# Sliding-window attention woven into a chain of matrix products: all of a group's attention products moved into one place

## The chip, the cores and the metric

The kernel runs on one core of a Trainium2 chip. The metric is the device time of one execution in microseconds (us). The core has five engines with queues of their own: PE (TensorE, the matrix products; the trace lists its weight loads apart, as PEld), DVE (VectorE), ACT (ScalarE), POOL (GpSimd) and SP (SyncE, which here only issues transfers). An engine takes its instructions in the order in which the program wrote them, and waits at one until what it needs is there.

## What is computed

The reference, cut to what matters:

```python
# q, k, v: (4, 8, 576, 64); window 64
scores = q @ k.T / 8
scores = where((rel >= 0) & (rel < 64), scores, -1e9)
attn = exp(scores - max); attn = attn / (sum(attn) + 1e-9)
x = (attn @ v)                      # as (2304, 512)
x = ((x @ w1) * (x @ w2) @ w3) @ w_out          # d_ff 1024
h = x @ w_in; out = (h * sigmoid(h)) @ w_out2   # d_ff 2048
```

## The kernel before

The 2304 tokens are 18 blocks of 128 queries, and the 8 heads are 4 pairs: 72 groups of attention, one for 128 queries and two heads. Three blocks of queries make a block of 384 tokens for the products that follow, of which there are six.

A group goes through these steps. `load_qk` and `load_v` have SP fetch its operands. `prep_qk` and `prep_v` (ACT, POOL, DVE) split them into a high and a low part in fp32r; the first 17 groups (`plain`) skip this and multiply in fp32. `scores` is three products on PE (one for a plain group) into the one PSUM tile `s`, followed by two reductions on DVE (line 275, which also mask). `exps` is two exponentials on ACT (line 286). `normalise` is three DVE operations (lines 294, 296, 298). `transposes` is three products on PE into the one PSUM tile `t` (line 308). `split_t` takes them out of PSUM: one ACT copy (line 314) for a plain group, else two kinds of ACT casts and two kinds of DVE subtractions (lines 318 to 323). `values` is three products on PE (lines 335 to 337, or 343 and 344) into the PSUM tile `o`, after which the result goes to the tile `xr`: one ACT copy (line 338) for a plain group, else two ACT copies, two DVE additions and one POOL addition (lines 347 to 351).

`half(h)` issues half a group's work: the even half 2g and the odd half 2g+1. The halves are spread over the other work by hand: `phase_w` (weights are converted from 64-bit words and `w3 @ w_out` is formed, PE line 476) issues the first 28 between its matrix products, and `phase_a` (the products `ab`, line 504, and `x`, line 524) issues one before each unit of 12 products, 24 units for each block of 384 tokens. So one group comes every two units. In `phase_w` steps of the conversion stand between the halves (`steps_to`), and `fill` puts single conversion steps of DVE between a half's own.

`split_x(blk, c)` makes the high and low parts of a fourth of `xr` (three groups) for the products of the next block; in `phase_a` it is called after the halves of units 17, 19, 21 and 22, and from the second block on both of its operations are DVE's. SP's transfers stand in one order too: a `load_v` that waits for a buffer holds up the loads of weight words (line 107) behind it.

The last phases (the products `h` and `o` of the second feed-forward network) hold no attention.

Of the kernel before, what the change touches and what calls it, by code (L numbers as in the profile page):

```python
# [9 lines left out]
F32 = mybir.dt.float32  # L10
# [4 lines left out]
ALU = mybir.AluOpType  # L15
# [27 lines left out]
def tile_window_attention_ffn(ctx, tc, qkv, vp, mask, ident, w1, w2, w3t, w_out, w_in, w_out2, out):  # L43
# [7 lines left out]
    nc = tc.nc  # L51
# [4 lines left out]
    att = late.enter_context(tc.tile_pool(name="att", bufs=2, side="right"))  # L56
    psa = late.enter_context(tc.tile_pool(name="psa", bufs=1, space=PSUM))

    def f32(ap):
        return ap.bitcast(F32)  # L60
# [91 lines left out]
    def loads_to(n):  # L152
        while done["load"] < min(n, len(line)):
            if line[done["load"]]:
                line[done["load"]].load()
            done["load"] += 1
# [29 lines left out]


    NG = NU * NPAIR
    LAST_HALF = 2 * NG + 2
    qk_raw, v_raw, qk_st, v_st, s_st, p_st = {}, {}, {}, {}, {}, {}  # L190
    pt = {}

# [9 lines left out]
    def plain(g):  # L202


        return g < PLAIN

    def place(g):
        blk, r = divmod(g, 3 * NPAIR)
        return blk * 3 + r % 3, r // 3
# [90 lines left out]
    def transposes(g):  # L300

        x = sm[g % 2]
        t_ps = psa.tile([128, 384], F32, name=f"t{g}", tag="t")
        x = x.rearrange("p h n -> p (h n)")
        for i, at in enumerate((0, 256, 128)):
            nc.tensor.transpose(t_ps[:, i * 128 : i * 128 + 128], x[:, at : at + 128], id_sb)  # L308
        return t_ps

    def split_t(g, t_ps):
        if plain(g):
            p_st[g] = p_w[g % 2]
            nc.scalar.copy(out=p_st[g], in_=t_ps[:, 0:320])
            return
        b, a = pt[g % 2, 1], pt[g % 2, 0]
        own, before = t_ps[:, 0:256].rearrange("p (h n) -> p h n", h=2), t_ps[:, 256:320]
        nc.scalar.copy(out=b[:, :, 0, :], in_=own)
        for h, hs in HEADS:
            nc.scalar.copy(out=a[hs, h, 0], in_=before[hs])  # L320
        nc.vector.tensor_tensor(out=b[:, :, 1, :], in0=own, in1=f32(b[:, :, 0, :]), op=ALU.subtract)
        for h, hs in HEADS:
            nc.vector.tensor_tensor(out=a[hs, h, 1], in0=before[hs], in1=f32(a[hs, h, 0]), op=ALU.subtract)

    def values(g):
        u, c = place(g)
        r = u % 3 * 128

        tag = "z" if done["step"] == len(line) and g % 2 else "o"
        o_ps = psa.tile([128, 2, 2, 128], F32, name=f"o{g}", tag=tag)  # L330
        if plain(g):


            v, p, o = v_p[g % 3], p_st.pop(g), o_ps[:, 0, 0]
            nc.tensor.matmul(o, lhsT=v[:, 0:128], rhs=p[:, 0:128], start=True, stop=False)
            nc.tensor.matmul(o, lhsT=v[:, 64:192], rhs=p[:, 128:256], start=False, stop=False)
            nc.tensor.matmul(o[:, 0:64], lhsT=v[:, 192:320], rhs=p[:, 256:320], start=False, stop=True)
            nc.scalar.copy(out=xr[:, c, r : r + 128], in_=o)
            return
        vhl = v_st.pop(g)  # L340
        b, a = pt[g % 2, 1], pt[g % 2, 0]
        for h in range(2):
            nc.tensor.matmul(o_ps[:, h], lhsT=vhl[:, h], rhs=b[:, h], start=(h == 0), stop=False)  # L343
        nc.tensor.matmul(o_ps[:, :, :, 0:64], lhsT=vhl[:, 2], rhs=a, start=False, stop=True)  # L344
        o_ps = o_ps.rearrange("p h t n -> p h (t n)")
        t = att.tile([128, 256], F32, name=f"ot{g}", tag="ot", bufs=1)
        nc.scalar.copy(out=t[0:64], in_=o_ps[64:128, 0, :])
        nc.scalar.copy(out=t[64:128], in_=o_ps[0:64, 1, :])
        nc.vector.tensor_tensor(out=t[0:64], in0=o_ps[0:64, 0, :], in1=t[0:64], op=ALU.add)
        nc.vector.tensor_tensor(out=t[64:128], in0=o_ps[64:128, 1, :], in1=t[64:128], op=ALU.add)  # L350
        nc.gpsimd.tensor_tensor(out=xr[:, c, r : r + 128], in0=t[:, 0:128], in1=t[:, 128:256], op=ALU.add)  # L351

    def half(h):


        g, odd = divmod(h, 2)
        if not odd:
            t_ps = transposes(g - 1) if 1 <= g <= NG else None
            if g < NG:
                scores(g)  # L360
            if t_ps is not None:
                split_t(g - 1, t_ps)
            if g < NG:
                exps(g)
        else:
            if g < NG:
                normalise(g)
            if 1 <= g <= NG:
                values(g - 1)
            for x in (g + 1, g + 2):  # L370
                if x - g == (1 if plain(x - 2) else 2):
                    prep_qk(x)
            if g < NG:
                prep_v(g)

            for x in range(g + 2, g + 5):
                if g < (x - 2 if plain(x - 2) else x - 4):
                    break
                load_qk(x)
            for x in range(g + 1, g + 4):  # L380
                if g < (x - 2 if plain(x - 3) else x - 3):
                    break
                load_v(x)

    halves = [0]

    def halves_to(n):
        while halves[0] < min(n, LAST_HALF):
            half(halves[0])
            halves[0] += 1  # L390
# [10 lines left out]
    def phase_w():  # L401
# [57 lines left out]
        acc, split_done = {}, set()  # L459
        for s in range(16):  # L460
            sw, j = divmod(s, 8)
            loads_to(ready[s + 2] + (3 if s > 1 else 0))
            if j == 0:
                for i in range(4):
                    acc[i] = accumulator(f"accw{sw}_{i}", [128, 512])
            for part in range(2):
                first = ready[s + 1 if s else 0]
                steps_to(first + (ready[s + 2] - first) * (part + 1) // 2, (nc.vector, nc.gpsimd), 3)
                halves_to(min(W_HALVES, 2 + W_HALVES * (2 * s + part + 1) // 32))
                for c in range(4):  # L470
                    if halves[0] >= 6 * c + 8 and (0, c) not in split_done:
                        split_done.add((0, c))
                        split_x(0, c)
                fill(3)
                for i in (0, 1) if part == 0 else (2, 3):
                    nc.tensor.matmul(  # L476
                        acc[i], lhsT=w3x[s % 7][:, i * 128 : (i + 1) * 128], rhs=wo[:, j],
                        start=(j == 0), stop=(j == 7),
                    )
                    if j == 7:  # L480
                        n = sw * 4 + i
                        wp[n] = slot(f"wp{n}", f"w{16 + n}", [2, 512], F32R)
                        split(wp[n][:, 0], wp[n][:, 1], acc[i], "act", "dve")
# [58 lines left out]
    with tc.manual_schedule():  # L542
        xr = slot("xr", "xr", [4, NB])
# [39 lines left out]
        for first, last in ((0, 3), (3, 7), (7, 11), (11, 16)):  # L583
# [6 lines left out]
            for key, src in chunks:  # L590
                tag = tags.pop(0)
# [68 lines left out]
        for i in range(1, len(jobs) + 1):  # L660
            if i < len(jobs):
                j, f = jobs[i]
# [93 lines left out]
```

## Time and profile before

| | |
|---|---|
| median of the runs | 884.69 us (the other near it: 883.5) |
| the profiled execution | 884.13 us, span 882.3 us |
| granted TensorE clock, mean | 0.997 of full speed |
| PE busy | 856.0 us (97% of the span) |
| DVE, ACT, POOL busy | 480.7, 491.0, 430.6 us |

The time outside the span is 884.13 - 882.3 = 1.8 us. The first weights and operands arrive at some 7 us; `phase_w` with its 28 halves lasts to about 104 us, the five blocks with attention to about 425 us, and the sixth block and the second network make up the rest. Busy shares are means over these stages, which have different limits.

### The profile page before, as it was taken

What the parts mean: (1) busy time and instruction counts of PE and PEld (TensorE: products, weight loads), DVE (VectorE), ACT (ScalarE), POOL (GpSimd) and SP (SyncE); (2) the same over time, 40 slices, a digit from 0 to 9 for tenths busy, and PEclk for the clock granted to TensorE, in tenths of its full rate; (3) what the DMA queues carried; (4) which work ended last, traced back from release to release, by engine and by line L of the source; (5) the groups of instructions that cost most, each with busy time, mean ns of one, the idle gap of its engine ahead of it and who ended that gap; (6) DMA issues with size and microseconds to landing.
All of it is one profiled execution on the core that took longest, in us unless ns stands there. A gap on an engine that the chain in (4) does not pass through costs nothing.

```text
span 882.3 us, 13255 instructions
## 1 busy us (share of the span) xinstructions
PE 856.0 (97%) x4362; PEld 737.0 (84%) x4362; DVE 480.7 (54%) x1202; ACT 491.0 (56%) x1219; POOL 430.6 (49%) x474
## 2 busy tenths in 40 slices
PE   4998999999999999999999999999999999999997
PEld 2454689999999999999999888888888888888896
DVE  5889888878888888888365886111111111111111
ACT  5778677788787788787475775222222222222322
POOL 4558476466466466465395787222322232222222
PEclk9999999999999999999999999999999999999999
DMA  8888423333432323331477500200020001000100
GB/s 286 295 251 262 134 79 99 125 99 100 127 94 90 126 90 100 119 99 50 182 277 261 202 0 1 77 20 0 1 89 7 0 1 51 22 0 1 48 1 25
DMA packets 43205, 85.84 MB, mean 97 GB/s; under 512 B 4864, under 2 KB 22528, under 8 KB 43136
## 3 DMA queue, kind: packets, MB, share of 16 engines
q1 hardware_dynamic: 37088, 75.55, 26.4%
q10 hardware_dynamic: 6048, 9.44, 2.9%
q8 instruction: 35, 0.57, 0.3%
q14 instruction: 34, 0.28, 0.1%
HBM read 75.53 MB, written 9.44 MB: 96 GB/s over the span
## 4 chain that ended last, share of the span: by engine, by line
PE 86%; DVE 2%; POOL 1%; issue 1%; ACT 0%; DMA 0%; POOLq 0%; SPq 0%; DVEq 0%
PE h L627 23%; PE o L646 22%; PE ab L504 21%; PE x L524 11%; PE t L308 2%; PE o L343 2%; PE s L265 1%; PE s L269 1%; PE accw L476 1%; PE o L344 1%; POOL klo L244 1%; DVE cv_b L128 0%; DVE cv_z L125 0%; DVE rs L294 0%; PE s L261 0%
## 5 line engine op out<-in xcount | busy, mean ns | idle before, releaser
L82 POOL TENSOR_TENSOR g<-sg,g 128x512 fp32r<-128x512 f32 (+1 forms) x80 | 94.8, 1185 | 250.0 <-ACT g L79 237.3
L627 PE MATMUL h<-x2t,hl 128*128 128x512 f32 (+1 forms) x960 | 213.4, 371 | 0.0
L646 PE MATMUL o<-hl,g 128*128 128x512 f32 x864 | 211.2, 392 | 0.4 <-ACT g L79 0.3
L633 DVE TENSOR_TENSOR sg<-h,sg 128x512 f32<-128x512 f32 (+1 forms) x80 | 51.1, 638 | 288.5 <-ACT sg L632 288.5
L627 PEld LDWEIGHTS h<-x2t,hl 128*128 128x128 f32 x960 | 169.4, 188 | 33.8
L646 PEld LDWEIGHTS o<-hl,g 128*128 128x128 f32 x864 | 160.9, 188 | 35.9 <-ACT g L79 0.8
L632 ACT ACTIVATE sg<-h 128x512 f32<-128x512 f32 (+1 forms) x80 | 44.4, 555 | 195.4 <-PE h L627 195.4
L504 PE MATMUL ab<-xa,hl 128*128 128x384 f32 x576 | 117.1, 338 | 0.0
L504 PE MATMUL ab<-xb,hl 128*128 128x384 f32 x576 | 115.6, 335 | 0.0
L504 PEld LDWEIGHTS ab<-xb,hl 128*128 128x128 f32 x576 | 101.4, 188 | 0.0
L504 PEld LDWEIGHTS ab<-xa,hl 128*128 128x128 f32 x576 | 99.8, 188 | 0.8
L351 POOL TENSOR_TENSOR xr<-ot 128x128 f32<-128x128 f32 x55 | 33.2, 603 | 118.5 <-DVE ot L350 116.5
L132 POOL TENSOR_TENSOR cv_b<-cv_b,cv_r 128x512 int32<-128x512 int32 x48 | 73.6, 1534 | 26.8 <-DVE cv_b L128 11.2
L79 ACT CAST g<-sg 128x512 fp32r<-128x512 f32 (+1 forms) x80 | 46.3, 579 | 63.5 <-DVE sg L633 61.8
L286 ACT ACTIVATE sm<-sm,nm 128x192 f32<-128x192 f32 x144 | 64.4, 448 | 17.7 <-DVE nm L275 16.6
L244 POOL TENSOR_TENSOR klo<-qk,qkhi 64x192 fp32r<-64x192 f32 x110 | 70.1, 637 | 5.7 <-ACT qkhi L240 1.5
L524 PE MATMUL x<-p,wp 128*128 128x384 f32 x360 | 69.6, 335 | 0.0
L524 PEld LDWEIGHTS x<-p,wp 128*128 128x128 f32 x360 | 62.2, 188 | 0.1
L125 DVE TENSOR_SCALAR cv_z<-cv_b 128x512 int32<-128x512 int32 x72 | 49.4, 686 | 17.0 <-ACT cv_b L114 16.6
L114 ACT ACTIVATE cv_b<-words 128x512 f32<-128x512 f32 x72 | 48.2, 670 | 11.5 <-DMA words<-in_w_out 5.6
L128 DVE SCALAR_TENSOR_TENSOR cv_b<-words,cv_z 128x512 int32<-128x512 int32 x72 | 49.4, 686 | 3.5 <-issue 0.5
L275 DVE CUSTOM_DVE_ANT_0 sm<-s,mask_sb 128x192 f32<-128x192 f32 x144 | 45.7, 354 | 6.6 <-PE s L261 3.6
(82 smaller groups left out, 1258.9 us busy)
## 6 DMA issues: line engine op xcount, KB each, us to landing
qk<-in_qkv SPq DMA_DIRECT2D x55, 384.0 KB, 3.1
words<-in_w_out SPq DMA_DIRECT2D x24, 512.0 KB, 8.4
words<-in_w3t SPq DMA_DIRECT2D x16, 512.0 KB, 6.2
words<-in_w SPq DMA_DIRECT2D x16, 512.0 KB, 6.2
words<-in_w_in SPq DMA_DIRECT2D x16, 512.0 KB, 6.8
v<-in_qkv SPq DMA_DIRECT2D x55, 96.0 KB, 2.7
x2d<-x2s ACTq DMA_DIRECT2D x24, 192.0 KB, 1.9
out_x<-osb ACTq DMA_DIRECT2D x18, 256.0 KB, 2.1
```

Of the source, the lines that this page charges most:

```text
L82: (nc.vector if eng_lo == "dve" else nc.gpsimd).tensor_tensor(out=lo, in0=src, in1=f32(hi), op=ALU.subtract)
L114: nc.scalar.activation(out=f32(self.b), in_=f32(self.high), func=AF.Copy, scale=2.0**-112)
L125: nc.vector.tensor_scalar(out=self.z, in0=b, scalar1=3, scalar2=None, op0=ALU.logical_shift_left)
L128: nc.vector.scalar_tensor_tensor(out=b, in0=self.high, scalar=-0x80000000, in1=self.z, op0=ALU.bitwise_and, op1=ALU.bitwise_or)
L132: nc.gpsimd.tensor_tensor(out=x, in0=b, in1=self.r, op=ALU.add)
L244: nc.gpsimd.tensor_tensor(out=k_lo[g % 2][hs, h * 192 : h * 192 + 192], in0=t[hs, n], in1=f32(hi[hs, n]), op=ALU.subtract)
L286: nc.scalar.activation(out=x, in_=x, func=AF.Exp, scale=-1.0, bias=nm[:, h : h + 1], accum_out=rs[:, h : h + 1])
L504: nc.tensor.matmul(acc, lhsT=w[:, l, fs], rhs=x[k // 2][:, k % 2, r, :], start=(k == 0 and n == 0), stop=(k == 3 and n == 2),)
L524: nc.tensor.matmul(acc, lhsT=wp[f][:, l, o * 128 : (o + 1) * 128], rhs=p[f][:, r, :], start=(f == 0 and n == 0), stop=(f == 7 and n == 2),)
L627: nc.tensor.matmul(acc, lhsT=weights["in", f // 4, k][:, l, fs], rhs=x[:, k, r, :], start=(k == 0 and i == 0), stop=(k == 3 and i == 2),)
L633: nc.vector.tensor_tensor(out=sg, in0=acc, in1=sg, op=ALU.mult)
L646: nc.tensor.matmul(oacc[t], lhsT=g[:, l, t * 128 : (t + 1) * 128], rhs=weights["out", f][:, r, :], start=(f == 0 and i == 0), stop=(f == 1 ...
```

## The change

In the even half 2g the order becomes: the values' products of group g-2, the scores of group g, the transposes of group g-1. `values` no longer issues what takes its result out of PSUM but gives it back as a function, which the half calls behind `split_t` and ahead of `exps`. The odd half has no products left. Values of a group come one half later than before, so there is one half more in all, a `load_v` of a plain group is issued one group later, and `split_x` in `phase_w` is called one half later.

```diff
-    LAST_HALF = 2 * NG + 2
+    LAST_HALF = 2 * NG + 3
@@ values(g)
-            nc.scalar.copy(out=xr[:, c, r : r + 128], in_=o)
-            return
+            return lambda: nc.scalar.copy(out=xr[:, c, r : r + 128], in_=o)
...
+        def total():
+            t = att.tile([128, 256], F32, name=f"ot{g}", tag="ot", bufs=1)
+            nc.scalar.copy(out=t[0:64], in_=o_ps[64:128, 0, :])
+            nc.scalar.copy(out=t[64:128], in_=o_ps[0:64, 1, :])
+            nc.vector.tensor_tensor(out=t[0:64], in0=o_ps[0:64, 0, :], in1=t[0:64], op=ALU.add)
+            nc.vector.tensor_tensor(out=t[64:128], in0=o_ps[64:128, 1, :], in1=t[64:128], op=ALU.add)
+            nc.gpsimd.tensor_tensor(out=xr[:, c, r : r + 128], in0=t[:, 0:128], in1=t[:, 128:256], op=ALU.add)
+
+        return total
@@ half(h)
         if not odd:
-            t_ps = transposes(g - 1) if 1 <= g <= NG else None
+            out_of = values(g - 2) if 2 <= g <= NG + 1 else None
             if g < NG:
                 scores(g)
-            if t_ps is not None:
-                split_t(g - 1, t_ps)
+            if 1 <= g <= NG:
+                split_t(g - 1, transposes(g - 1))
+            if out_of is not None:
+                out_of()
             if g < NG:
                 exps(g)
         else:
             if g < NG:
                 normalise(g)
-            if 1 <= g <= NG:
-                values(g - 1)
...
-                if g < (x - 2 if plain(x - 3) else x - 3):
+                if g < (x - 1 if plain(x - 3) else x - 3):
                     break
                 load_v(x)
@@ phase_w
-                    if halves[0] >= 6 * c + 8 and (0, c) not in split_done:
+                    if halves[0] >= 6 * c + 9 and (0, c) not in split_done:
```

On PE, near the start of a block's units in `phase_a` (`t` transposes, `s` scores, `o` values, `ab` the unit's products), there stood before:

```order
L504 MATMUL ab_14_2442<-xa_1644,hl 128x384 x6
L504 MATMUL ab_14_2442<-xb_1645,hl 128x384 x6
L343 MATMUL o_2460<-pt_977,vhl_2399 128x256 x2
L344 MATMUL o_2460<-pt_975,vhl_2399 128x4x64
L504 MATMUL ab_15_2482<-xa_1644,hl 128x384 x6
L504 MATMUL ab_15_2482<-xb_1645,hl 128x384 x6
L308 MATMUL t_2499<-id_sb,sm_73 128x128 x3
L265 MATMUL s_2503<-qkhi_2394 128x192 x2
L269 MATMUL s_2503<-klo_74,qkhi_2394 128x384
L524 MATMUL x_1_0_2498<-p_1888,wp_557 128x384 x3
```

and there stands now:

```order
L507 MATMUL ab_14_2442<-xa_1634,hl 128x384 x6
L507 MATMUL ab_14_2442<-xb_1635,hl 128x384 x6
L507 MATMUL ab_15_2472<-xa_1634,hl 128x384 x6
L507 MATMUL ab_15_2472<-xb_1635,hl 128x384 x6
L342 MATMUL o_2489<-pt_971,vhl_2389 128x256 x2
L343 MATMUL o_2489<-pt_969,vhl_2389 128x4x64
L265 MATMUL s_2493<-qkhi_2384 128x192 x2
L269 MATMUL s_2493<-klo_74,qkhi_2384 128x384
L308 MATMUL t_2501<-id_sb,sm_73 128x128 x3
L527 MATMUL x_1_0_2488<-p_1878,wp_556 128x384 x3
```

The values' products have left the place between two units, and the transposes stand behind the scores. In `phase_w` the same happens around the products `accw`.

On DVE, at units 22 and 23 of a block (`sm` the reductions, `pt` the subtractions of `split_t`, `xb` the last `split_x` of the block, `rs` and `sm` the normalising, `ot` the additions behind the values, `qkhi` the preparation), there stood before:

```order
L275 ISA sm_73,nm_1822<-s_1818,mask_sb 128x192
L275 ISA nm_1822 128x1
L321 TENSOR_TENSOR pt_977<-t_1814,pt_977 128x2x128
L323 TENSOR_TENSOR pt_975<-t_1814,pt_975 64x64 x2
L81 CAST xb_1645<-xr 128x384
L82 TENSOR_TENSOR xb_1645<-xr,xb_1645 128x384
L294 TENSOR_SCALAR rs_1823<-rs_1823 128x2
L296 RECIPROCAL rs_1823<-rs_1823 128x2
L298 TENSOR_TENSOR sm_73<-sm_73,rs_1823 128x384
L349 TENSOR_TENSOR ot_1855<-o_1851,ot_1855 64x256
L350 TENSOR_TENSOR ot_1855<-o_1851,ot_1855 64x256
L247 TENSOR_TENSOR qkhi_1861<-qk_1717,qkhi_1861 64x256
```

and there stands now:

```order
L275 ISA sm_73,nm_1812<-s_1808,mask_sb 128x192
L275 ISA nm_1812 128x1
L321 TENSOR_TENSOR pt_971<-t_1816,pt_971 128x2x128
L323 TENSOR_TENSOR pt_969<-t_1816,pt_969 64x64 x2
L350 TENSOR_TENSOR ot_1826<-o_1804,ot_1826 64x256
L351 TENSOR_TENSOR ot_1826<-o_1804,ot_1826 64x256
L81 CAST xb_1635<-xr 128x384
L82 TENSOR_TENSOR xb_1635<-xr,xb_1635 128x384
L294 TENSOR_SCALAR rs_1813<-rs_1813 128x2
L296 RECIPROCAL rs_1813<-rs_1813 128x2
L298 TENSOR_TENSOR sm_73<-sm_73,rs_1813 128x384
L247 TENSOR_TENSOR qkhi_1851<-qk_1707,qkhi_1851 64x256
```

The two additions have moved from behind the normalising to ahead of `split_x`, which reads what POOL makes of them.

On SP, early in `phase_w` (`qk` and `kp` are scores' operands, `vp` the values', `words` weights), there stood before:

```order
L219 DMA qk_236<-in_qkv 128x128
L223 DMA kp_77<-in_qkv 64x192 x2
L229 DMA vp_78<-in_vp 128x320
L107 DMA words<-in_w_out 128x1024
L107 DMA words<-in_w3t 128x1024
L107 DMA words<-in_w_out 128x1024
```

and there stands now:

```order
L219 DMA qk_231<-in_qkv 128x128
L223 DMA kp_77<-in_qkv 64x192 x2
L107 DMA words<-in_w_out 128x1024
L107 DMA words<-in_w3t 128x1024
L107 DMA words<-in_w_out 128x1024
L107 DMA words<-in_w3t 128x1024
L107 DMA words<-in_w_out 128x1024
L107 DMA words<-in_w3t 128x1024
L219 DMA qk_288<-in_qkv 128x128
L223 DMA kp_76<-in_qkv 64x192 x2
L229 DMA vp_78<-in_vp 128x320
```

The transfer `vp` has gone behind six loads of words and the next group's scores' operands.

## Rows read from the trace of the kernel before

**Rows 1.** Waits of PE from 104 to 430 us.

```profile
PE t L308 <- DVE sm L298: 1.0, 1, 1.0
```

**Rows 2.** Timeline of PE: start, us, line; four groups' transposes, the first and last of 53.

```profile
140.49 0.49 PE L308 MATMUL t<-id_sb,sm 128*128 128x128 f32 x3
...
372.02 0.49 PE L308 MATMUL t<-id_sb,sm 128*128 128x128 f32 x3
...
377.29 0.49 PE L308 MATMUL t<-id_sb,sm 128*128 128x128 f32 x3
...
419.84 0.49 PE L308 MATMUL t<-id_sb,sm 128*128 128x128 f32 x3
```

**Rows 3.** Timeline of PE and DVE around one group's products, among the `ab` units.

```profile
253.84 0.49 PE L308 MATMUL t<-id_sb,sm 128*128 128x128 f32 x3
...
254.57 1.20 PE L504 MATMUL ab<-xa,hl 128*128 128x384 f32 x6
...
256.28 0.44 DVE L323 TENSOR_TENSOR pt<-t,pt 64x64 fp32r<-64x64 f32 x2
...
256.65 0.39 PE L343 MATMUL o<-pt,vhl 128*128 128x256 f32 x2
...
257.06 1.24 PE L504 MATMUL ab<-xa,hl 128*128 128x384 f32 x6
```

**Rows 4.** Timeline of DVE, ACT and POOL over the same stretch; in brackets the idle time before.

```profile
254.20 0.56 DVE L512 TENSOR_TENSOR a<-ab,a 128x384 f32<-128x384 f32 x1
...
254.79 0.51 ACT L79 CAST p<-a 128x384 fp32r<-128x384 f32 x1 [0.82 <-DVE a L512]
...
255.21 0.36 ACT L318 CAST pt<-t 128x256 fp32r<-128x256 f32 x1
...
255.93 0.46 ACT L286 ACTIVATE sm<-sm,nm 128x192 f32<-128x192 f32 x1
...
256.35 1.02 POOL L82 TENSOR_TENSOR p<-a,p 128x384 fp32r<-128x384 f32 x1
...
256.95 0.44 DVE L294 TENSOR_SCALAR rs<-rs 128x2 f32<-128x2 f32 x1 [0.23 <-ACT sm L286]
...
257.44 0.37 ACT L347 COPY ot<-o 64x256 f32<-64x256 f32 x1
...
258.27 0.42 DVE L349 TENSOR_TENSOR ot<-o,ot 64x256 f32<-64x256 f32 x1
...
259.08 0.42 DVE L247 TENSOR_TENSOR qkhi<-qk,qkhi 64x256 fp32r<-64x256 f32 x1
...
259.21 0.61 POOL L351 TENSOR_TENSOR xr<-ot 128x128 f32<-128x128 f32 x1 [1.84 <-DVE ot L350]
...
259.53 0.56 DVE L512 TENSOR_TENSOR a<-ab,a 128x384 f32<-128x384 f32 x1
```

**Rows 5.** Waits of PE from 7 to 104 us: us in total, times, longest.

```profile
PE o L335 <- ACT pw L314: 2.8, 2, 1.9
```

**Rows 6.** Waits of DVE from 7 to 104 us.

```profile
DVE sm L275 <- PE s L261: 3.2, 3, 1.6
```

**Rows 7.** Timeline of SP's queue in early `phase_w`.

```profile
21.84 0.33 SPq L229 DMA_DIRECT2D vp<-in_vp  x1
```

**Rows 8.** Timeline of ACT in early `phase_w`.

```profile
25.28 0.42 ACT L314 COPY pw<-t 128x320 f32<-128x320 f32 x1 [1.27 <-PE t L308]
...
30.34 0.68 ACT L114 ACTIVATE cv_b<-words 128x512 f32<-128x512 f32 x1 [1.74 <-DMA words<-in_w3t]
```

**Rows 9.** Timeline at units 22 to 24 of the third block, DVE and PE.

```profile
299.76 0.36 DVE L81 CAST xb<-xr 128x384 fp32r<-128x384 f32 x1
...
301.02 0.56 DVE L298 TENSOR_TENSOR sm<-sm,rs 128x384 f32<-128x384 f32 x1
...
302.16 0.49 PE L308 MATMUL t<-id_sb,sm 128*128 128x128 f32 x3
```

**Rows 10.** Timeline of DVE among `x` units, the same operation of normalising.

```profile
236.26 0.16 DVE L294 TENSOR_SCALAR rs<-rs 128x2 f32<-128x2 f32 x1
```

More of the change, by code (lines that the diff above doesn't have):

```diff
@@ L345, in values @@
         o_ps = o_ps.rearrange("p h t n -> p h (t n)")
[L346 to L351, printed above, removed]
+        def total():
[6 more added lines that the diff above has]
+        return total
     def half(h):
```

## The prediction

> **What bounds the kernel now.** Three views were read: the granted clock and busy shares (PE is busy nearly throughout, at full clock), then the waits by stage, then the timeline of one group after another. The waits alone mislead. From 104 to 430 us they show PE with hardly a wait [rows 1], so that PE seems to run at its own pace. The timeline says otherwise. From 140.49 to 419.84 us there are 53 starts of transposes, 52 periods of a group, and their mean is 279.35 / 52 = 5.37 us, yet single ones take 377.29 - 372.02 = 5.27 us [rows 2]. All hold the same products: so PE can go at 5.27 us, and mostly doesn't. What holds it shows in one group: the subtractions that make the values' operand end at 256.28 + 0.44 = 256.72 us, and the values' first product had started at 256.65 [rows 3]. PE waits inside the values' three products, where the modelled ends of its rows hide it.
>
> Why the operand is late shows in the same stretch [rows 4]. DVE's product `a` (254.20) releases ACT's cast `p` (254.79, idle 0.82 for it); behind that stand ACT's casts of the transposes (255.21), the exponentials (255.93), then DVE's normalising (256.95), its two additions (258.27), the subtraction `qkhi` (259.08), and the next product `a` at 259.53. 259.53 - 254.20 = 5.33 us with no gap in it: a loop over DVE and ACT, through their order, sets the period, and PE follows, tied by the values. So a change of PE's order can gain where it unties PE from this loop, up to 5.37 - 5.27 a group.
>
> The other stage that matters is `phase_w` (to some 104 us), where PE, DVE, ACT and the transfers wait for each other in turn [rows 5 to 8]. Behind 430 us nothing changes.
>
> **The values' operand.** Its casts and subtractions are now read a whole unit later, some two microseconds after they are done. The wait inside the values goes: 279.35 - 52 x 5.27 = 5.3 us at most by these rows (5.27 may hide a little itself: 5.9 us with 5.26). What is late next is the loop, and it changes too. The two copies out of `o` come before the exponentials on ACT: two by 0.37, with their latencies some 0.77 (257.44 to the next cast). The two additions leave the stretch behind the normalising, 259.08 - 258.27 = 0.81, and stand in front of it while DVE waits for the exponentials anyway. New loop: 5.33 - 0.81 + 0.77 = 5.29 us. That is a trifle above 5.27, and PE is tied to it only by the transposes, whose operand the normalising makes. Their spare time before: they start at 253.84 + 5.33 = 259.17, the normalising was done by 258.27, so 0.9. Now they stand behind the values (257.06 - 256.65 = 0.41) and the scores (some 0.4 of 254.57 - 253.84 = 0.73), 0.8 later, for 0.77 that the exponentials are later: still 0.9. Eight groups among the `ab` units at 0.02 more each use little of it. I take -4.5 us, some of the 5.3 given back to the new loop; bounds -5.9 and 0.
>
> **The end of a block.** The values of a block's last group now come in the half right ahead of its last `split_x`. On DVE this puts the additions (0.81) and the wait for POOL's addition (0.61 and two hand-overs, 0.2) ahead of the cast, which so far could start at 299.76; from there to the end of the normalising it is 301.02 + 0.56 - 299.76 = 1.82 [rows 4, 9]. Sum: 299.76 + 0.81 + 0.81 + 1.82 = 303.2 us, while the transposes, due at 302.16 before, are due at 302.16 + 0.8 = 302.96. That is 0.25 us late; with the copies' 0.77, which push the additions too, at most 1.0. I take 0.7 for each of the four block ends with a next group: +2.8 us; bounds 0 and 4 x 1.2 = 4.8.
>
> **phase_w.** Before, scores stood behind transposes, which wait for DVE's normalising, and DVE's next reduction waits for those scores: a round trip. Now scores go first. What this can free: DVE's 3.2 us for scores [rows 6]; the values' 2.8 us for ACT's copy, which is a group old now [rows 5]; and SP, which stood at a `vp` load until the values had freed its buffer at 21.84 us [rows 7], ahead of word loads for one of which ACT idled 1.74 us at 30.34 [rows 8]. DVE, with the conversion, is the fuller engine here, so I count its gains, not PE's: 3.2 + 1.74 = 4.9, rounded down to 4.7 as a ceiling, and half of the transfer's part taken, 3.2 + 0.9 = 4.1. Against it stand four `split_x`: their cast on DVE now follows a half whose copy into `xr` comes behind transposes (0.49) and ACT's copy out of them (0.42 [rows 8]); less the reductions beside it, some 0.4 each, 1.6. Sum -2.5; bounds -4.7 and +1.6.
>
> **The rest.** PE's wait of 1.0 us in the first block [rows 1] is one for the normalising, and the transposes come 0.8 later: -0.7 (bounds -1.0 and 0). The number of instructions stays the same on every engine, but for one half more, which is a place and no work. [...]
>
> **Sum.** Against the profiled execution's 884.13 us (the median of the runs is 884.69): -4.5 + 2.8 - 2.5 - 0.7 = -4.9, so 879.2 us.
>
> **The rivals.** (a) `phase_w` gains nothing, since DVE's conversions and the transfers pace it whatever PE does, and the `split_x` waits remain: 884.1 - 4.5 + 2.8 + 1.6 - 0.7 = 883.3. For it: DVE's waits for scores are three only [rows 6]. Against: the rows of SP and ACT.
> (b) All terms at their good ends: 884.1 - 5.9 - 4.7 - 1.0 = 872.5. For it: the block ends may be covered by DVE's idle time for casts.
> (c) Slower than before: the new loop becomes the bound. Its place is the first operation of the normalising, which takes 0.16 us where POOL is idle [rows 10] and 0.44 where POOL's `p` runs until 257.37 [rows 4]; it ends with POOL's operation. POOL's addition into `xr` now starts just when the normalising does. If all of its 0.61 us comes on top of 0.17, the loop grows by 0.17 + 0.61 - 0.44 = 0.34 to 5.63, 0.36 above PE's 5.27. Over eight groups that is 2.9 us, from the third group on (0.9 spare) paid by PE: 2.0 us for each of 4.5 blocks, 9.0. With the values' full gain: 884.1 - 5.3 + 2.8 - 2.5 - 0.7 + 9.0 = 887.4. It decides from a loop of 5.27 + 0.9 / 8 = 5.38 us on. [...]
> (d) The change doesn't untie anything: PE waits at the transposes as long as it did at the values, the periods stay: 884.1 + 2.8 - 2.5 - 0.7 = 883.7. Against it: the 0.9 us of spare time.
>
> **How the numbers follow.** Chances: forecast 0.45, (a) 0.18, (b) 0.10, (c) 0.14, (d) 0.13. The likeliest is 879.2 us. The range 872 to 888 takes in all five times; what is left out is that two bad ends meet, or that a wait arises that I don't see. Faster by over 2% (about what a measurement of this kernel can tell from no change) would be below 867.0 us, more than all good ends together: 0.03. Slower by over 2% is above 902.4; the loop would have to grow to some 6.1 us: 0.03. Within 2%: 0.94.
>
> **What would show it.** In the profile after, group periods of 5.25 to 5.30 us among the `ab` and `x` units, and the values' three products in 0.35 us, show the first term; a period of 5.33 or more there refutes it. A gap ahead of the transposes of a block's first units, by DVE's normalising, shows the second. The third is read from when the first `ab` product starts, at some 104 us before: 101 to 102 after. For (c), look at the duration of line 294 and whether transposes wait in the later units of a block, not in the first. The forecast is wrong if PE's weight loads make the merged place dearer than the two apart, which no row here shows, or if ACT, with two more copies ahead of its exponentials, falls behind.

## The result, and the profile after

The changed kernel takes 894.4 us (median of five runs, 893.34 to 897.04) against 883.86 us for the kernel before, timed beside it: a ratio of 1.0124, 95% interval 1.0103 to 1.0145. It is slower by some 10 us where 4.9 us less was forecast, and outside the range of 872 to 888. The profiled execution of after has a span of 891.5 us, that of before 882.3.

Lines in helpers and units have moved a little: `ab` is line 507 (504 before), the product `a` line 515 (512), the additions into `ot` lines 350 and 351, POOL's addition into `xr` line 352, the values' products lines 342 and 343. Lines 244 (`klo`), 247 (`qkhi`), 294, 298 and 308 have kept their numbers.

First come PE's waits from 100 to 430 us: us in total, times, longest. They answer to [rows 1], where the wait for the normalising was 1.0 us in all.

```profile
PE t L308 <- DVE sm L298: 10.8, 5, 2.5
PE s L265 <- DVE qkhi L247: 1.7, 1, 1.7
PE ab L507 <- POOL hl L144: 1.1, 1, 1.1
```

Next, PE's timeline of after: start, us, line. The rows are the first transposes among the `ab` units, then four groups at the end of a block and behind it, then three groups late in that next block's `ab` units, one with its values and scores ahead of it. They answer to [rows 2, 3, 9].

```profile
98.50 0.49 PE L308 MATMUL t<-id_sb,sm 128*128 128x128 f32 x3
...
231.62 0.52 PE L308 MATMUL t<-id_sb,sm 128*128 128x128 f32 x3
...
239.61 0.87 PE L308 MATMUL t<-id_sb,sm 128*128 128x128 f32 x3 [2.52 <-DVE sm L298]
...
246.23 0.49 PE L308 MATMUL t<-id_sb,sm 128*128 128x128 f32 x3
251.48 0.49 PE L308 MATMUL t<-id_sb,sm 128*128 128x128 f32 x3
...
267.26 0.49 PE L308 MATMUL t<-id_sb,sm 128*128 128x128 f32 x3
...
271.75 0.39 PE L342 MATMUL o<-pt,vhl 128*128 128x256 f32 x2
271.98 0.28 PE L343 MATMUL o<-pt,vhl 128*128 128x256 f32 x1
272.10 0.37 PE L265 MATMUL s<-qkhi 128*128 128x192 f32 x2
...
272.75 0.52 PE L308 MATMUL t<-id_sb,sm 128*128 128x128 f32 x3
...
278.33 0.52 PE L308 MATMUL t<-id_sb,sm 128*128 128x128 f32 x3
```

Three things are to be seen. The phase that makes the weights ends earlier: 98.50 against 103.88 us. Inside the blocks a period is 5.25 to 5.28 us for some groups behind a block's start (251.48 - 246.23 = 5.25) and then 278.33 - 272.75 = 5.58 us, more than the 5.33 before, although the values' three products no longer wait: they take 272.10 - 271.75 = 0.35 us. And at the block end a period is 239.61 - 231.62 = 7.99 us, and the one behind it 246.23 - 239.61 = 6.62. All four block ends are alike (7.98, 7.99, 7.98, 7.99).

The long period behind the wait shows in the granted clock. The table by stretches has, behind the stretch and its length, the busy time of PE, its weight loads, DVE, ACT and POOL, then the granted clock, DMA share and GB/s.

```profile
172.00:180.00 8.00, 7.62 (x48) 7.64 (x49) 6.68 (x23) 5.59 (x18) 3.33 (x5) 1.00 0.32 98
239.00:246.30 7.30, 6.69 (x34) 6.71 (x35) 5.31 (x16) 3.91 (x13) 1.80 (x3) 0.77 0.24 67
374.90:381.80 6.90, 6.85 (x34) 6.87 (x35) 4.78 (x15) 3.87 (x12) 1.80 (x3) 0.75 0.25 75
```

Behind two of the four block ends (239 and 375 us) the mean granted clock was 0.77 and 0.75, with 0.50 from 240 to 242 and from 376 to 378 us; behind the other two (172 and 308) it stayed at 1.00, after waits of the same 2.52 us.

Where the time went, by the starts of transposes at the borders of the stages in both timelines:

| border | before | after | after - before | the stage's own part |
|---|---|---|---|---|
| first `ab` group | 103.88 | 98.50 | -5.38 | -5.38 (`phase_w`) |
| first `x` group, block 0 | 151.16 | 147.75 | -3.41 | +1.97 |
| first `ab` group, block 1 | 173.09 | 172.38 | -0.71 | +2.70 (block end) |
| first `x` group, block 1 | 216.10 | 214.95 | -1.15 | -0.44 |
| first `ab` group, block 2 | 237.81 | 239.61 | +1.80 | +2.95 (block end) |
| first `x` group, block 2 | 280.50 | 283.63 | +3.13 | +1.33 |
| first `ab` group, block 3 | 302.16 | 308.04 | +5.88 | +2.75 (block end) |
| first `x` group, block 3 | 344.86 | 350.61 | +5.75 | -0.13 |
| first `ab` group, block 4 | 366.54 | 374.95 | +8.41 | +2.66 (block end) |
| first `x` group, block 4 | 409.28 | 419.72 | +10.44 | +2.03 |

The four `x` stages with their block ends lose 11.1 us, the `ab` stages of blocks 1 to 4 lose 2.8, which is what the two periods at the lower granted clock take there (6.62 - 5.27 and 6.83 - 5.27, together 2.9), block 0's `ab` stage loses 2.0, and `phase_w` gains 5.4. Behind the last border the changed kernel's trace is 1.2 us shorter than the other, so that the spans differ by 9.2.

Why the groups take 5.58 us shows in the timeline of DVE and POOL over one of them (in brackets the idle time before), which answers to [rows 4].

```profile
267.80 0.56 DVE L515 TENSOR_TENSOR a<-ab,a 128x384 f32<-128x384 f32 x1
...
271.32 0.46 POOL L352 TENSOR_TENSOR xr<-ot 128x128 f32<-128x128 f32 x1 [1.32 <-DVE ot L351]
271.33 0.48 DVE L294 TENSOR_SCALAR rs<-rs 128x2 f32<-128x2 f32 x1
271.84 0.17 DVE L296 RECIPROCAL rs<-rs 128x2 f32<-128x2 f32 x1
272.04 0.56 DVE L298 TENSOR_TENSOR sm<-sm,rs 128x384 f32<-128x384 f32 x1
272.47 1.34 POOL L244 TENSOR_TENSOR klo<-qk,qkhi 64x192 fp32r<-64x192 f32 x2 [0.69 <-ACT qkhi L240]
272.63 0.72 DVE L247 TENSOR_TENSOR qkhi<-qk,qkhi 64x256 fp32r<-64x256 f32 x1
273.38 0.56 DVE L515 TENSOR_TENSOR a<-ab,a 128x384 f32<-128x384 f32 x1
```

273.38 - 267.80 = 5.58, the period. One operation has grown for which the forecast has no term: `qkhi`, line 247, takes 0.72 us where it took 0.42 [rows 4]. POOL's `klo` began 0.16 us ahead of it. Before, `klo` stood on POOL's queue behind the addition into `xr`, which waits for DVE's two additions, and these came right ahead of line 247 [rows 4]; so DVE's operation began first, 45 of 45 times from 170 to 432 us. Now that addition is done half a group earlier, and `klo` waits for ACT's cast alone, while line 247 still stands behind the normalising on DVE.

At the block end the same lag meets the split. The rows are DVE's and POOL's from the last scores of a block on.

```profile
235.60 0.43 DVE L351 TENSOR_TENSOR ot<-o,ot 64x256 f32<-64x256 f32 x1
236.11 0.46 POOL L352 TENSOR_TENSOR xr<-ot 128x128 f32<-128x128 f32 x1 [2.76 <-DVE ot L351]
236.53 1.25 POOL L244 TENSOR_TENSOR klo<-qk,qkhi 64x192 fp32r<-64x192 f32 x2
236.60 0.73 DVE L81 CAST xb<-xr 128x384 fp32r<-128x384 f32 x1 [0.57 <-POOL xr L352]
237.37 0.83 DVE L82 TENSOR_TENSOR xb<-xr,xb 128x384 fp32r<-128x384 f32 x1
237.86 0.78 POOL L82 TENSOR_TENSOR vhl<-v,vhl 128x192 fp32r<-128x192 f32 x1
238.12 0.55 DVE L294 TENSOR_SCALAR rs<-rs 128x2 f32<-128x2 f32 x1
238.70 0.17 DVE L296 RECIPROCAL rs<-rs 128x2 f32<-128x2 f32 x1
238.90 0.56 DVE L298 TENSOR_TENSOR sm<-sm,rs 128x384 f32<-128x384 f32 x1
```

The cast takes 0.73, the subtraction 0.83 and line 294 0.55, where 0.36, 0.56 and 0.17 are the shortest that the same lines show. Together that is 1.02 us, on top of a DVE that already comes late out of `x` groups of 5.54 to 5.58 us.

### The profile page after: what moved, and what is told of

Read it like the earlier page. It is cut to its first block, busy times and chain, and to the rows that moved or that the text cites. A ratio compares the mean times of both kernels' runs of the same rounds, so it can differ in the third digit from the quotient of the medians.

```text
span 891.5 us, 13228 instructions
## 1 busy us (share of the span) xinstructions
PE 856.3 (96%) x4362; PEld 738.3 (83%) x4362; DVE 494.5 (55%) x1202; ACT 481.8 (54%) x1219; POOL 431.9 (48%) x474
## 4 chain that ended last, share of the span: by engine, by line
PE 58%; issue 9%; ACT 9%; DVE 7%; POOL 5%; DMA 0%; POOLq 0%; ACTq 0%; SPq 0%; DVEq 0%
PE h L630 22%; PE o L649 22%; PE ab L507 9%; PE x L527 4%; POOL klo L244 2%; ACT sm L286 2%; DVE qkhi L247 2%; DVE rs L294 1%; ACT ot L349 1%; ACT ot L348 1%; ACT pt L318 1%; ACT pt L320 1%; DVE sm L275 1%; ACT qkhi L240 1%; POOL vhl L82 1%
## 5 line engine op out<-in xcount | busy, mean ns | idle before, releaser
L507 PE MATMUL ab<-xa,hl 128*128 128x384 f32 x576 | 120.9, 345 | 0.0
L244 POOL TENSOR_TENSOR klo<-qk,qkhi 64x192 fp32r<-64x192 f32 x110 | 75.1, 682 | 33.3 <-ACT qkhi L240 29.1
L352 POOL TENSOR_TENSOR xr<-ot 128x128 f32<-128x128 f32 x55 | 25.7, 467 | 103.9 <-DVE ot L351 103.9
L286 ACT ACTIVATE sm<-sm,nm 128x192 f32<-128x192 f32 x144 | 64.5, 450 | 11.8 <-DVE nm L275 10.8
L125 DVE TENSOR_SCALAR cv_z<-cv_b 128x512 int32<-128x512 int32 x72 | 49.4, 687 | 16.0 <-ACT cv_b L114 14.8
L308 PE MATMUL t<-id_sb,sm 128*128 128x128 f32 x216 | 36.7, 279 | 19.3 <-DVE sm L298 16.0
L308 PEld LDWEIGHTS t<-id_sb,sm 128*128 128x128 f32 x216 | 24.8, 141 | 33.4 <-issue 13.0
```

Of the source, the lines that this page charges most:

```text
L125: nc.vector.tensor_scalar(out=self.z, in0=b, scalar1=3, scalar2=None, op0=ALU.logical_shift_left)
L244: nc.gpsimd.tensor_tensor(out=k_lo[g % 2][hs, h * 192 : h * 192 + 192], in0=t[hs, n], in1=f32(hi[hs, n]), op=ALU.subtract)
L286: nc.scalar.activation(out=x, in_=x, func=AF.Exp, scale=-1.0, bias=nm[:, h : h + 1], accum_out=rs[:, h : h + 1])
L507: nc.tensor.matmul(acc, lhsT=w[:, l, fs], rhs=x[k // 2][:, k % 2, r, :], start=(k == 0 and n == 0), stop=(k == 3 and n == 2),)
```

## The experiments

Two theories stood against each other: A, the block end costs more than forecast, since the split stands ahead of the normalising there; B, the loop over DVE itself has grown. Then, for B: because `klo` runs beside `qkhi`, or because of something else in the new order. All runs were timed beside the kernel before.

| run | us | ratio to before, 95% interval |
|---|---|---|
| e1_split_late | 888.34 | 1.0067 [1.0048, 1.0085] |
| e2_out_odd | 880.91 | 0.9978 [0.9963, 0.9994] |
| e3_w_only | 876.48 | 0.9925 [0.9909, 0.9942] |
| e4_no_klo | 877.23 | 0.9937 [0.9920, 0.9955] |
| e5_klo_late | 890.41 | 1.0082 [1.0063, 1.0100] |
| e6_klo_split_late | 881.89 | 0.9989 [0.9974, 1.0005] |
| e7_mix | 873.71 | 0.9893 [0.9874, 0.9912] |
| e8_values_odd | 882.13 | 0.9987 [0.9976, 0.9999] |
| e9_before_klo_first | 884.21 | 1.0011 [1.0001, 1.0020] |
| e10_klo_behind_sub | 875.70 | 0.9910 [0.9886, 0.9934] |
| e11_klo_behind_sub_split_late | 876.48 | 0.9908 [0.9890, 0.9927] |

### Block end or loop: e1, e2

e1 is the changed kernel with a block's last split where the other three stand:

```diff
-                    if blk + 1 < NBLK and o == 3 and f == 0:
-                        split_x(blk + 1, 3)
-                    if blk + 1 < NBLK and o < 3 and f == 4:
+                    if blk + 1 < NBLK and f == 4:
```

> The changed kernel with one edit: the last split_x of a block is called after the half of unit 23, no longer after that of unit 22 (so behind the normalising, and a half after the values it reads). Theory A (the loss sits at the block ends: DVE meets split_x and the wait for POOL's addition ahead of the normalising, PE waits 2.5 us four times, and twice its clock falls to half for another 1.4): the four waits and the two slow spells go, 4 x 2.5 + 2 x 1.4 = 12.8 us, so 894.4 - 12.8 = 881.6, 880 to 885. Theory B (the loop over DVE and ACT, longer by the two copies, sets the pace; the block end only collects what the loop owes): DVE's lag shows up one or two groups later, 889 to 893.

888.34 us, above A's range and 0.7 under B's: the waits at the block ends and the periods of 6.62 and 6.83 us behind two of them are gone (no two of DVE's normalisings from 172 to 419 us are more than 5.58 apart), but periods are 5.54 to 5.58 most of the time, and the kernel is still slower than before. So B describes the periods, and A is not the whole.

e2 has e1's splits, and the result is taken out of `o` in the odd half, behind the normalising, as before; the products stay together in the even half:

```diff
-            if out_of is not None:
-                out_of()
...
+            if g in kept:
+                kept.pop(g)()
```

> PE's new order, but the result of the values leaves PSUM in the odd half behind the normalising, where it stood before the change (last split_x at unit 23 as in e1, those of phase_w one half later still). Theory B (the place of the copies and additions on ACT and DVE makes the loss): the loop is the old one, 5.33 us among the ab units and 5.44 among the x units, phase_w keeps its gain of 5.4 us: 884 - 5.4 = 878.6, 877 to 881. Theory A without B: the same as e1, 880 to 885. If PE's order itself were dear, it would stay above 888.

880.91 us, 7.4 under e1 with the same work on every engine. This lies in B's range by two misses that cancel: the loop was expected at 5.33 and 5.44 us, but the periods are 5.24 to 5.28 inside the stages, and the first phase's gain was expected to stay. The reason for the short periods stands in DVE's and POOL's timeline of e2:

```profile
285.28 0.43 DVE L351 TENSOR_TENSOR ot<-o,ot 64x256 f32<-64x256 f32 x1
285.63 0.42 DVE L247 TENSOR_TENSOR qkhi<-qk,qkhi 64x256 fp32r<-64x256 f32 x1
285.79 0.58 POOL L352 TENSOR_TENSOR xr<-ot 128x128 f32<-128x128 f32 x1 [1.78 <-PE t L308]
```

With the addition back ahead of `klo`, line 247 begins first and takes 0.42 us again. But e2 loses most of the first phase's gain (first `ab` transposes at 102.74): there PE waits 6.7 us for ACT's copy into `xr` (line 338), which the changed kernel doesn't show. So the place at which the result is taken out of `o` is what gains in `phase_w` and what costs in the blocks.

### The first phase alone: e3

The new order up to group 14, where `phase_w` ends, and before's order from there:

```diff
-            out_of = values(g - 2) if 2 <= g <= NG + 1 else None
+            t_ps = transposes(g - 1) if SW < g <= NG else None
+            out_of = values(g - 2) if 2 <= g <= SW else None
...
+            if SW <= g <= NG:
+                values(g - 1)()
```

> The new order for groups below 14 alone, that is in phase_w; from there on the order and places of the kernel before. All theories agree that phase_w gained 5.4 us (first ab unit at 98.5 for 103.9) and that the rest lost 15: 884 - 5.4 = 878.5. If the gain is given back in the first block, where DVE still converts (2.0 of the 5.4 were gone at the end of its ab units in the changed kernel), 881 to 884.

876.48 us, 6.4 under before and 2 under the 878.5 expected. The first `ab` transposes come at 98.19 us, 5.7 earlier than before, and the whole gain lasts to the end.

### The suspected neighbour taken away: e4

POOL's `klo` is left out from group 19 on, so a part of the scores' product is missing:

```diff
-        for h, hs in HEADS:
+        for h, hs in HEADS if g < PLAIN + 2 else ():
```

> The changed kernel without POOL's two subtractions klo from group 19 on (the low parts of k are stale there, so that this part of the product is left out). Theory C (DVE's qkhi subtraction takes 0.72 us for 0.42 and the first split_x cast 0.65 for 0.36 because POOL's klo now runs beside them; this makes the loop 5.58 and 5.55 us): both fall back, loops of 5.28 or PE's own 5.27, block ends less late: 894.4 - 8 = 886, 882 to 888. Theory A alone, with no part for POOL: 892 to 895.

877.23 us, a larger gain than expected. Periods are 5.24 to 5.28. At the block end, of PE's timeline:

```profile
292.71 0.49 PE L308 MATMUL t<-id_sb,sm 128*128 128x128 f32 x3
...
298.61 0.52 PE L308 MATMUL t<-id_sb,sm 128*128 128x128 f32 x3 [0.47 <-DVE sm L298]
```

5.90 us, 0.63 over a plain period, where the prediction took 0.7. So with `klo` gone the prediction's own terms come out; but less work is also less work, and the next runs keep all of it.

### The neighbour moved: e5, e6

In e5 `klo` stands behind the low part of the values' operand on POOL from group 24 on; e6 is e5 with e1's split.

```diff
-        for h, hs in HEADS:
-            n = slice(384 + h * 192, 576 + h * 192)
-            nc.gpsimd.tensor_tensor(
-                out=k_lo[g % 2][hs, h * 192 : h * 192 + 192], in0=t[hs, n], in1=f32(hi[hs, n]), op=ALU.subtract
-            )
+        behind.append((g, t, hi))
+        if g < 24:
+            klo()
...
                 prep_v(g)
+            klo()
```

> The changed kernel with one thing moved: from group 24 on, POOL's two subtractions klo of the scores' operand stand behind POOL's low part of the values' operand instead of ahead of it; all of the work is still done. Theory 'overlap' (DVE's subtraction L247 is stretched from 0.42 to 0.71 us because klo now runs beside it, and this 0.3 us, with the DVE lag behind it, makes the loop 5.55 to 5.58 and the block ends 7.98): L247 back to 0.42 to 0.45, group periods 5.25 to 5.30, block ends shorter by 1 us or more, total 877 to 882. Rival 'amount' (POOL simply has too much to do between its waits, wherever klo stands): periods stay at 5.5 to 5.6, total 890 to 895. Rival 'moved only' (klo now runs beside another DVE operation and stretches that one instead): L247 is 0.42 but another DVE row grows by about 0.3, total 888 to 893.

> The same as the run before, with the last channel's split of the next block half a block later too (at the place where the others stand). Theory 'overlap' with a block-end cost that is the split's own: the block-end period falls to the others' 5.25 to 5.5 at all four ends, no fall of the granted clock behind them, total 873 to 878, 3 to 5 us below the run before. Rival 'the block end was only the lag': once the loop no longer lags, the split's place is worth less than 1 us, and the two runs are equal.

e5 is a miss: 890.41 us. Among the `ab` units all is as theory "overlap" had it (line 245, which is 247 here, 0.42 us, periods 5.25 to 5.27). Among the `x` units POOL's next operation has taken the place of `klo`:

```profile
290.70 0.92 POOL L82 TENSOR_TENSOR vhl<-v,vhl 128x192 fp32r<-128x192 f32 x1
...
291.19 0.72 DVE L245 TENSOR_TENSOR qkhi<-qk,qkhi 64x256 fp32r<-64x256 f32 x1
...
291.58 1.46 POOL L255 TENSOR_TENSOR klo<-qk,qkhi 64x192 fp32r<-64x192 f32 x2
...
291.94 0.64 DVE L81 CAST xa<-xr 128x384 fp32r<-128x384 f32 x1
292.61 0.84 DVE L82 TENSOR_TENSOR xa<-xr,xa 128x384 fp32r<-128x384 f32 x1
```

DVE needs 5.57 us a group there, PE's periods stay at 5.26, DVE loses 0.3 us on PE with each, and the block ends cost 8.0 us as in the changed kernel: the rival "moved only" comes nearest for this stage, though what has changed is POOL's operation beside line 245 and not DVE's operation beside `klo`. In e6, with the split later, the ends are gone and the `x` periods are 5.56: 881.89 us, above the 873 to 878 expected, and 8.5 under e5.

### Later without together: e8; three orders in one kernel: e7

e8 is before with the values a whole group later at their old place in the odd half (and e1's splits, which it needs):

```diff
-                values(g - 1)
+                values(g - 2)
```

> The kernel before with one thing changed: the values' products are those of two groups back, a whole group later in the odd half at the place where they stood, not in the even half; so 'later' without 'all products together'. If the operand's wait is all that there is to gain and merging is worth nothing, this has the periods of 5.25 to 5.30 and a total of 879 to 882, like the run with the result's way out in the odd half. If the merging itself saves time on TensorE, periods stay at 5.3 to 5.45, total 882 to 885. If the later result makes the block ends wait, periods of 5.26 with block ends of 6.5 to 8, total 883 to 890.

882.13 us, between two of the expectations, with periods of 5.26 to 5.29 and, from the middle of the `ab` stages into the `x` stages, 5.31 to 5.35; line 247 stays at 0.42. The mean period from block 1 to the first `x` group of block 4 is 5.31 us, against 5.37 before and 5.26 in e11, so "later" alone takes more than half of the values' wait away. Its first phase is slower than before's (first `ab` transposes at 105.7 us), and block 0's `ab` stage is too (49.4 us, before 47.3), which hides that in the total.

e7 takes the changed order up to group 14, before's up to 24, and e2's from there on.

> Three orders in one kernel: up to group 14 (the phase that makes the weights) that of the changed kernel, from there to group 24 that of the kernel before, and from 24 on the changed kernel's order with the result taken out of PSUM in the odd half behind the normalising multiplication, and with the splits late. If the gain of the first phase (5.4 us at the first product of the first block) and that of the third order (periods 5.26 in place of 5.33 to 5.44, about 3 us over 50 groups) add up: 871 to 875. If the first phase's gain is given back later, because the blocks then wait for something else (their weights or inputs): 876 to 880.

873.71 us, as expected: the gains of the first phase and of the blocks add up, and this beats both kernels.

### The neighbour put into the kernel before: e9

On POOL alone, `klo` stands ahead of the addition into `xr` from group 24 on:

```diff
+            sum_of = values(g - 1) if 1 <= g <= NG else None
...
                     prep_qk(x)
+            if sum_of is not None and g >= 24:
+                sum_of()
```

> The kernel before with one exchange on POOL's queue, from group 24 on: the two klo subtractions stand ahead of the result's addition xr instead of behind it; every product, copy and DVE operation stays where it was. Theory 'overlap': klo no longer waits for the two additions on DVE, so it starts with DVE's subtraction L247 and stretches it from 0.42 to 0.65 us or more; the periods of the loop, 5.33 in the blocks' first part and 5.44 in the second, become 5.4 to 5.6, and the total is 886 to 894. Rival 'the new order of the products is at fault': L247 may be longer, but the periods stay within 0.03 of before's and the total within 2 us of 883. Rival 'the late addition xr': the later xr makes the split of the next block's input and the block ends wait, seen as waits of the DVE cast for xr over 0.5 us, with periods inside the blocks unchanged; 884 to 888.

884.21 us, 1.0011 [1.0001, 1.0020]: the theory as written fell. `klo` did run beside line 247 through its whole length, and line 247 stayed at 0.42 us. DVE and POOL of e9:

```profile
285.21 0.41 DVE L247 TENSOR_TENSOR qkhi<-qk,qkhi 64x256 fp32r<-64x256 f32 x1
285.21 1.54 POOL L244 TENSOR_TENSOR klo<-qk,qkhi 64x192 fp32r<-64x192 f32 x2 [1.63 <-ACT qkhi L240]
285.65 0.64 DVE L81 CAST xa<-xr 128x384 fp32r<-128x384 f32 x1
286.33 0.84 DVE L82 TENSOR_TENSOR xa<-xr,xa 128x384 fp32r<-128x384 f32 x1
```

Here both begin together, and DVE's is not longer; the cast that begins while `klo` runs takes 0.64 us, where it took 0.50 before, and three `x` periods of a block are 5.53 to 5.63 in place of 5.44, while the one behind them falls from 5.46 to 5.29. So overlap is not what counts here, but which of the two begins first. The new theory "start": an operation of DVE with its operands in SBUF that begins while POOL is inside one of its own takes longer, and one that is already running does not. The 0.28 us that the next expectation names for this are not a constant; the last section shows what sets them.

### Who begins first, with all work kept: e10, e11

e10 is the changed kernel, and from group 24 on POOL copies one column of what line 247 has written before it starts `klo`:

```diff
+        if g >= 24:
+            nc.gpsimd.tensor_copy(out=seen[64:128], in_=f32(hi[64:128, 128:129]))
```

> The changed kernel, and from group 24 on POOL copies one column of what DVE's subtraction L247 writes before it starts klo, so klo can't run while L247 does; all work is kept and one small copy a group is added. Theory 'start' (a DVE operation with both operands in SBUF that starts while POOL is inside an operation takes 0.28 us more; one that is already running is not stretched): L247 falls from 0.71 to 0.42, the groups' periods from 5.55 to 5.58 to 5.25 to 5.30, the block ends from 7.98 to 6 or 7, total 878 to 884. Rival 'amount' (POOL's work or memory traffic as such slows the loop): L247 shorter, but another DVE row or PE's wait for POOL's p and q grows by as much, periods over 5.5, total 889 to 896.

> The same with the last channel's split half a block step later, at the place of the others. Theory 'start': periods 5.25 to 5.30 at the block ends too, and with the first phase's gain of 5 us the total is 874 to 878, 3 to 7 us under the run before. Rival 'the block end was the lag alone': no more than 1 us under the run before.

e10 takes 875.70 us (0.9910 of before, where the changed kernel is 1.0124), 18.7 under the changed kernel, with one small copy a group more. That is below the expected 878 to 884. PE's wait for the normalising from 100 to 420 us is down from 10.8 us to

```profile
PE t L317 <- DVE sm L307: 0.7, 1, 0.7
```

and DVE and POOL show why (line 249 is 247 here, line 254 `klo`):

```profile
284.57 0.42 DVE L249 TENSOR_TENSOR qkhi<-qk,qkhi 64x256 fp32r<-64x256 f32 x1
285.03 0.36 DVE L81 CAST xa<-xr 128x384 fp32r<-128x384 f32 x1
285.13 0.30 POOL L251 COPY seen<-qkhi 64x1 f32<-64x1 f32 x1 [1.41 <-DVE qkhi L249]
285.42 0.56 DVE L82 TENSOR_TENSOR xa<-xr,xa 128x384 fp32r<-128x384 f32 x1
285.49 1.61 POOL L254 TENSOR_TENSOR klo<-qk,qkhi 64x192 fp32r<-64x192 f32 x2
```

Now no operation of POOL runs when line 249 begins, the cast begins ahead of `seen` and the subtraction ahead of `klo`, and each takes its shortest time, 0.42, 0.36 and 0.56 us; it is `klo` that grows instead (1.61 for the two, against 1.25 among the `ab` units, at 264.17 and 269.63, where DVE's neighbours read PSUM), and nothing waits for `klo`. Periods are 5.24 to 5.28, block ends 5.50. e11, with the split later, takes 876.48: no gain over e10, so the rival "the block end was the lag alone" holds. The 2.7 us of a block end needed DVE's lateness: without it the split's early place costs 0.24 (e10).

## Why the prediction was wrong

The forecast's sum has no term for the preparation of `qkhi`, `klo` and `vhl`, and that is where it failed. The preparation is issued in the same half as before. But `klo` was held back by POOL's addition into `xr` ahead of it, and so began behind DVE's line 247; the change moved that addition away. Line 247 went from 0.42 to 0.71 us (median of 45), the split's cast in the `x` units from 0.50 to 0.65, and the loop came to 5.58 us. e10 shows this to be the cause: it restores that order with one small copy and keeps all other work, and the loss turns into a gain.

Point by point:

- **The values' operand, -4.5.** By the prediction's own sign (a period of 5.33 or more refutes it) the term did not come out in the changed kernel. The part on PE was right: the three products take 0.35 us and wait no more. The new loop was worked out as 5.29 us; e4 and e10 show 5.24 to 5.28 with the stretch gone, the changed kernel 5.54 to 5.58 with it. In e2, where the order on DVE and ACT is as it was, DVE's normalising still comes every 5.30 to 5.35 us among the `ab` units, while PE's periods are 5.26; it catches up among the `x` units, with 5.04 to 5.05.
- **The block ends, +2.8.** 0.7 each was forecast. It is 0.63 in e4 and 0.24 in e10 over a plain period of 5.26, and 2.7 in the changed kernel. What was missed is again the stretch: DVE comes late out of the `x` units, and the cast, the subtraction and line 294 begin inside POOL's operations. Two of the four waits were also followed by a granted clock of 0.77 and 0.75, with periods 1.35 and 1.56 us over 5.27, for which the prediction had no term.
- **`phase_w`, -2.5.** It gained 5.4 in this pair of traces (5.7 in e3). Single traces spread here: with the new order the first `ab` transposes come at 97.8 (e5) to 100.6 us (e11), with the old one at 103.1 (e9) and 103.9. The gains that were named came for the most part (DVE's wait for scores 3.2 to 0.7 us, PE's for ACT's copy 2.8 to 0.4, ACT's for words 7.6 to 6.0), while the 1.6 us set against them for the splits were 0.3: DVE's only such wait in that stretch, for ACT's copy into `xr`.
- **The rest, -0.7.** PE's wait for the normalising in the first block is 0.7 us in place of 1.0. And block 0's `ab` stage lost 2.0 us: PE waits 1.7 for line 247 and 1.1 for POOL's `hl` while conversions still run there. e3, with before's order there, doesn't have the loss; e8 has it (49.4 us for the stage, 49.3 in the changed kernel, 47.3 before) with the values later at their old place. So the products need not stand together for it, and later values alone bring a loss of this size; but why is open, since in e8 PE's waits there are others (2.5 for the normalising, 0.7 for `hl`).
- **The merged place on PE.** The forecast was to be wrong if it were dearer than the two apart. Nothing in the runs shows that: e10's plain periods, with the products together, are 5.24 to 5.28, and before's shortest, with them apart, is 5.27.
- **Rival (c), 887.4.** It had the right kind of effect, an operation of VectorE that takes longer and ends with one of POOL, at the wrong operation. Line 294 takes 0.48 beside the addition into `xr`, which lasts 0.46 there, against 0.44 beside `p` before [rows 4]: no difference that counts. The same question had to be asked of each of DVE's operations, not only of the one that the moved addition now meets: what does POOL begin earlier, once the moved operation is gone from ahead of it?

Without the stretch the forecast of 879.2 would have been 3.5 us too high, by e10's 875.70.

## What to carry to other kernels

When an operation is moved on a shared queue, look at what stood behind it: what it held back may begin earlier, and here that was worth more than the move. Between VectorE and GpSimd the order of two starts counted here for more than the amount of work: line 247 took 0.70 to 0.74 us where it began inside `klo` and 0.42 where it began first, and a dependency of one copy of 0.18 to 0.30 us, which set that order, took 18.7 us off the kernel. A change that gains in one phase and loses in another is best tried phase by phase: e3, e7 and e10 all keep the gain and drop the loss.

## What the runs showed of the hardware

**Operations of VectorE took longer by most of what one of GpSimd had left.** From 170 to 432 us of the changed kernel, line 247 began while `klo` was running 33 times and took 0.70 to 0.74 us; the 12 other times it took 0.42. In e9 it began ahead of `klo` or together with it 40 times and took 0.41 to 0.42 although `klo` ran beside it to the end. The five times that it began later there, with 0.20 to 0.30 us of one of `klo`'s two subtractions left, it took 0.48 to 0.59. So the added time is no fixed charge. It shows in these rows of the kernel before, where 285.82 + 0.57 - 286.11 = 0.28 us of the addition were left and the cast, 0.36 us alone, took 0.14 more:

```profile
285.82 0.57 POOL L351 TENSOR_TENSOR xr<-ot 128x128 f32<-128x128 f32 x1 [1.78 <-DVE ot L350]
286.11 0.50 DVE L81 CAST xa<-xr 128x384 fp32r<-128x384 f32 x1
```

Line 294, 0.17 us alone, took 0.27 more with 0.42 left [rows 4], 0.31 more with 0.45 left (at 271.33) and 0.38 more with 0.52 left (at 238.12). In the traces of the two kernels, from 140 to 432 us, 169 operations of lines 81, 82, 247 and 294 are longer than the shortest of their line by 0.13 to 0.41 us. All of them began inside an operation of POOL, and each time the added time is what was left of it, less 0.12 to 0.15 us; what this remainder is, the runs don't show. (`klo` counts as two operations here, since it is two subtractions.) The 0.28 us come back so often because 110 of them began with 0.40 to 0.44 left. In the changed kernel line 294 also began eight times within 0.01 us of the addition's recorded start and took 0.17 us; at that distance the records don't tell which of the two was first.

The operations that read PSUM show none of it: in the changed kernel, from 140 to 432 us, line 515 began inside `klo` 33 times and took 0.56 each time, as without it, and lines 321 and 323 began inside an operation of POOL 34 and 40 times and took 0.42 to 0.43 and 0.20 to 0.23, as elsewhere. Nor does the reciprocal of line 296: it began inside the addition 17 times and took 0.17 as elsewhere. It reads one operand, but so does the cast of line 81, which took up to 0.76 us; what sets the two apart, the runs don't show. Nor do they show by what mechanism the longer ones are held, only which of the two takes longer and, to within 0.15 us of the other's recorded end, until when.

**The clock fell after two of four equal waits.** In the changed kernel PE waited 2.52 us at each block end. Behind the ones at 172 and 308 us the granted clock was 1.00 and the periods 5.28 us; behind the ones at 239 and 375 us it was 0.77 and 0.75, and the periods 6.62 and 6.83. What tells them apart, the runs don't show.
